# First feed-forward network on pairs of fp16 halves instead of pairs of fp32r halves, scales worked out on the chip

## The chip, the cores and the metric

One core of one Trainium2 chip runs the whole program in one launch. The metric is device microseconds of that core; lower is better. Engines are named as in the profile: PE (TensorE matmuls), PEld (its weight loads), DVE (VectorE), ACT (ScalarE), POOL (GpSimd), SP (SyncE, which issues most DMAs).

## The reference, cut to what matters

```python
X = np.fft.rfft(x, axis=1)                       # x: 8 x 3072 x 256
y = np.fft.irfft(X * (filt_r + 1j*filt_i), n=3072, axis=1)
x = y.reshape(24576, 256)
h = x @ w_in                                     # w_in: 256 x 2048, float64
g = np.where(h >= 1, h, np.where(h <= -1, 0.0, (h + 1)**2 / 4))
x = (g @ w_out).astype(np.float32)               # w_out: 2048 x 256, float64
logits = x @ w_gate                              # 8 experts
e = argmax(logits); p = softmax(logits)[e]
out = p * (np.maximum(x @ w1[e], 0) @ w2[e])     # w1: 256 x 1024, w2: 1024 x 256 per expert
```

The filter is a Fourier transform along 3072 positions, the first network is dense over all 24576 tokens, and the second sends each token to one of eight experts.

## The kernel before, in words

**Three parts in time.** The first sequence's transform, alone, with the conversion of the first network's weights (0 to 126 us). Then 768 *units* of the first network, 48 blocks of 512 tokens times 16 slices of 128 hidden columns; beside the first 672 of them the transforms of the seven other sequences run in the gaps, one per 96 units, so that the last 96 units have none. From about 2720 us on the experts, in tiles of 256 tokens.

**Precision by pairs.** A number is split into a high part and a rest (`wih`, `wil` for the first weights, `woh`, `wol` for the second, `xh`, `xl` for the tokens, `gh`, `gl` for the activations), and a product is three matmuls: high by high, high by rest, rest by high. In the first network both parts are of type fp32r, four bytes; the experts do the same with fp16 parts (their weights' scale is worked out on the chip in `wscale`, and each token row has its own).

**A unit.** `l1` issues six matmuls of 512 columns into one of two PSUM tiles `hps` (L453). DVE clips the sum to -1..1 (`cl`, L456), ACT squares (L457), DVE takes the maximum of square and sum (`g`, L463), which frees `hps`; ACT rounds `g` to `gh` (L466), POOL subtracts to get `gl` (L467). Three units later `l2` multiplies by the second weights: eight matmuls of 264 columns with `gh`, four with `gl` (L478), 264 because the gate's eight columns are folded into `w_out`. After 16 units `finish` copies the sums out and DVE works out each token's scale and expert.

**Weights.** The float64 weights arrive as pairs of integers, a slice of both matrices per DMA pair (`cv_load`, 16 slices, two `raw` buffers). `cv_run` rebuilds fp32 numbers in eight DVE operations; ACT and POOL split them (`cv_in`, `cv_out`); a transposition, a copy and a small matmul fold in the gate. Slices 0 to 14 are placed in the transform's list of times, slice 15 in the list of events.

**What sets the order.** The code writes each piece of work under a time (`at`, for the first sequence) or under a half unit (`ev`); a scheduler then sets each engine's stream from the dependences. Engines run their streams in order and wait on semaphores. On PE nothing but the stream's order decides what is next.

Of the kernel before, what the change touches and what calls it, by code (L numbers as in the profile page):

```python
# [23 lines left out]
BLK = 512  # L24
# [8 lines left out]
CVA, CVN, CH, CS = 4, 15, -29, 4  # L33
# [95 lines left out]
def tile_kernel(ctx, tc, x, w_in, w_out, w_gate, w1, w2, cst, tab, fil, out):  # L129
# [27 lines left out]
    wih = wp.tile([128, 2, FF], F32R, name="wih")  # L157
    wil = wp.tile([128, 2, FF], F32R, name="wil")
    woh = wp.tile([128, NF, WO], F32R, name="woh")
    wol = wp.tile([128, NF, WO], F32R, name="wol")  # L160
# [4 lines left out]
    if True:  # L165
# [21 lines left out]

        def cv_run(f, i):
            if i == 0:
                ex = fp.tile([128, 512], I32, tag="cl", name="cvx")  # L190
                m = fp.tile([128, 512], I32, tag="g", name="cvm")
                r = fp.tile([128, 512], I32, tag="gh", name="cvr", bufs=4)
                w = fp.tile([128, 512 + E], F32, tag="row", name="cvw")
# [36 lines left out]
        def cv_lg(f):  # L230
            w, wt = cv[f]
            lg = psH.tile([128, 512], F32, tag="h", name="hps")
            for k in range(2):
                PE.matmul(lg[:, 0:E], lhsT=wt[:, k * 128:(k + 1) * 128], rhs=wg[:, k, :], start=k == 0, stop=k == 1)
            cv[f] = (w, lg)

        def cv_out(f):
            w, lg = cv.pop(f)
            V.tensor_copy(w[:, 512:512 + E], lg[:, 0:E])
            A.activation(woh[:, f, :], w[:, 256:512 + E], AF.Copy)  # L240
            G.tensor_tensor(wol[:, f, :], w[:, 256:512 + E], woh[:, f, :].bitcast(F32), op=ALU.subtract)
# [45 lines left out]
        def fft_unit(u, ha, sa, hb, sb, lag):  # L287
# [78 lines left out]
            def b_inv(g):  # L366
                tt = st.pop(("b", g))[0]
                yh, yl = st.pop(("q", g))
                p = ups(u)
                for i in range(2):  # L370
                    pi = p[0:96, i * D:(i + 1) * D]
                    if u:
                        mm(pi, tt[:, 0, i, 128:224], tt[:, 1, i, 128:224], yh[:, i], yl[:, i])
                    else:
                        PE.matmul(pi, lhsT=tt[:, 0, i, 128:224], rhs=yh[:, i], start=True, stop=False)
                        PE.matmul(pi, lhsT=tt[:, 0, i, 128:224], rhs=yl[:, i], start=False, stop=True)
                z = alt(u, g, [96, 2, D], "z", (qp, "ao"), (qp, "xi"), (qp, "xg"), (qp, "xr"))
                A.activation(z.rearrange("p q d -> p (q d)"), p[0:96], AF.Copy)
                SP.dma_start(s2v[8 * g:8 * g + 8].rearrange("(q p) s d -> (p s) q d", q=2), z)

            if u == 0:
# [6 lines left out]
                for f in range(CVN):  # L388
# [5 lines left out]
                    at(t, (cv_in, f), (cv_tr, f), (cv_ev, f), (cv_lg, f))  # L394
                    at(t + 1, (cv_out, f))
                for g in range(NG):
# [5 lines left out]
                    at(t + P0[12], (b_inv, g))  # L402
                for _, _, fs in sorted(todo):
# [42 lines left out]
        def l1(n):  # L446
# [75 lines left out]
        def route1(k, i):  # L522
# [5 lines left out]
            if i == 0:  # L528
# [10 lines left out]
                A.activation(ex, d, AF.Exp)  # L539
# [115 lines left out]
        for f in range(CVN, NF):  # L655
            h = CH + CS * (f - CVN)
            ev(h - 6, lambda f=f: cv_load(f))
            for i in range(4):
                ev(h, lambda f=f, i=i: cv_run(f, i))
            for fn in (cv_in, cv_tr, cv_ev, cv_lg, cv_out):  # L660
                ev(h + 1, lambda f=f, fn=fn: fn(f))
# [264 lines left out]
```

## Time and profile before

| | |
|---|---|
| median of 3 runs | 3791.17 us (3788.31 to 3793.49) |
| the profiled execution | 3793.5 us, all of it span (first to last instruction) |
| PE busy | 3651.2 us, 96% of the span |
| PEld, DVE, ACT, POOL busy | 86%, 64%, 50%, 49% |
| TensorE clock, mean over the span | 0.990 of full |

The profiled execution is one of the three runs, 2.3 us above their median. PE's busy time covers matmuls from start to modelled end, and these overlap; what one matmul costs in a stream is read from the distance of two starts. A row of the timeline is: start, duration, engine, line, operation, output <- inputs, and in brackets the idle time before it with what ended it.

### The profile page before, as it was taken

The page shows a single profiled execution, that of the slowest core. Times are in us where ns is not written, and L with a number is a line of the kernel's source. Part 1 is how long each engine was busy: PE and PEld are TensorE (multiplying, and loading weights), DVE is VectorE, ACT ScalarE, POOL GpSimd, SP SyncE. Part 2 cuts the span into 40 slices and gives each one's busy share as a digit, 9 for nine tenths or more (in the row PEclk, how much of TensorE's full clock was granted, in tenths as well). Part 3 has the DMA queues.
Part 4 walks back from the last instruction along what each step waited for, and adds up shares of the span by engine and source line. Part 5 has one row for each costly group of instructions (what it writes and reads, how often), then busy time and mean ns, then how long its engine had stood idle before and what let it go on. Part 6 is the DMA issues. An engine that isn't in the chain of part 4 may idle for free. (4 is left out here: it accounts for less than half of the span.)

```text
span 3793.5 us, 70055 instructions
## 1 busy us (share of the span) xinstructions
PE 3651.2 (96%) x26055; PEld 3267.4 (86%) x26055; DVE 2417.0 (64%) x4496; ACT 1900.6 (50%) x3376; POOL 1877.7 (49%) x1570
## 2 busy tenths in 40 slices
PE   6999999999999999999999999999999999999998
PEld 4788888888888888888888888898888888888887
DVE  7588768767876876777687677767643333333332
ACT  6556556656665665666566556544432222222222
POOL 3555565556556656555665556555432222222222
PEclk8999999999999999999999999999999999999999
DMA  9444434434443443444344334201122222222221
GB/s 289 133 133 137 127 122 144 133 101 136 136 130 108 143 129 115 125 136 122 124 139 126 114 106 149 87 23 66 47 69 53 52 51 52 52 52 51 51 52 52
DMA packets 326122, 395.01 MB, mean 104 GB/s; under 512 B 164047, under 2 KB 254415, under 8 KB 325264
## 3 DMA queue, kind: packets, MB, share of 16 engines
q1 hardware_dynamic: 277152, 279.90, 25.9%
q0 software_dynamic: 48624, 110.58, 9.7%
q8 instruction: 207, 3.39, 0.4%
q14 instruction: 139, 1.14, 0.1%
HBM read 439.70 MB, written 120.49 MB: 148 GB/s over the span
## 5 line engine op out<-in xcount | busy, mean ns | idle before, releaser
L467 POOL TENSOR_TENSOR gl<-g,gh 128x512 fp32r<-128x512 f32 x768 | 1024.7, 1339 | 787.3 <-ACT gh L466 722.8
L478 PE MATMUL yps<-woh,gh 128*128 128x264 f32 x3072 | 812.4, 286 | 2.7 <-ACT gh L466 2.2
L478 PE MATMUL yps<-wol,gh 128*128 128x264 f32 x3072 | 811.0, 285 | 0.0
L463 DVE TENSOR_TENSOR g<-cl,hps 128x512 f32<-128x512 f32 x768 | 524.2, 683 | 353.7 <-ACT cl L457 277.3
L466 ACT ACTIVATE gh<-g 128x512 fp32r<-128x512 f32 x768 | 483.3, 630 | 455.8 <-DVE g L463 436.7
L453 PE MATMUL hps<-xh,wih 128*128 128x512 f32 x1536 | 621.6, 405 | 56.1 <-DVE g L463 55.0
L795 DVE SCALAR_TENSOR_TENSOR hl<-mh,hh 128x512 f16<-128x512 f32 x388 | 268.2, 691 | 633.8 <-ACT hh L794 632.7
L457 ACT ACTIVATE cl<-cl 128x512 f32<-128x512 f32 x768 | 483.7, 630 | 365.4 <-DVE cl L456 308.6
L478 PE MATMUL yps<-woh,gl 128*128 128x264 f32 x3072 | 634.5, 287 | 11.6 <-POOL gl L467 11.1
L456 DVE TENSOR_SCALAR cl<-hps 128x512 f32<-128x512 f32 x768 | 525.2, 684 | 172.6 <-PE hps L453 170.5
L453 PE MATMUL hps<-xh,wil 128*128 128x512 f32 x1536 | 604.4, 393 | 0.0
L453 PE MATMUL hps<-xl,wih 128*128 128x512 f32 x1536 | 603.7, 393 | 0.0
L478 PEld LDWEIGHTS yps<-woh,gh 128*128 128x128 f32 x3072 | 579.1, 189 | 25.0 <-ACT gh L466 5.2
L478 PEld LDWEIGHTS yps<-wol,gh 128*128 128x128 f32 x3072 | 579.3, 189 | 17.6
L794 ACT ACTIVATE hh<-mh 128x512 f16<-128x512 f32 x388 | 231.4, 597 | 724.4 <-PE mh L789 715.0
L789 PE MATMUL mh<-xt,wslot 128*128 128x256 f16 x4656 | 572.1, 273 | 0.0
L812 PE MATMUL my<-wslot,hh 128*128 128x256 f16 x3104 | 529.2, 273 | 0.0
L478 PEld LDWEIGHTS yps<-woh,gl 128*128 128x128 f32 x3072 | 489.6, 189 | 40.5 <-POOL gl L467 19.3
L825 POOL DMA_INDIRECT out_dram<-o,me x194 | 191.8, 989 | 658.6 <-ACT o L822 536.8
L789 PEld LDWEIGHTS <-wslot 128*128 128x128 f16 x4656 | 455.0, 98 | 53.1 <-issue 0.3
L812 PE MATMUL my<-wslot,hl 128*128 128x256 f16 x1552 | 422.9, 273 | 0.0
L453 PEld LDWEIGHTS hps<-xh,wih 128*128 128x128 f32 x1536 | 289.9, 189 | 112.2 <-DVE g L463 75.4
(159 smaller groups left out, 4911.6 us busy)
## 6 DMA issues: line engine op xcount, KB each, us to landing
tf<-in_fil_dram SPq DMA_DIRECT2D x113, 512.0 KB
tt<-in_tab_dram POOLq DMA_DIRECT2D x112, 448.0 KB
wst<-in_w_dram SPq DMA_DIRECT2D x128, 256.0 KB
xi<-in_x_dram SPq DMA_DIRECT2D x48, 512.0 KB
scr<-ao SPq DMA_DIRECT2D x48, 512.0 KB
a<-scr SPq DMA_DIRECT2D x128, 192.0 KB
scr<-z SPq DMA_DIRECT2D x128, 192.0 KB
zt<-scr SPq DMA_DIRECT2D x48, 512.0 KB
```

Of the source, the lines that this page charges most:

```text
L453: PE.matmul(p, lhsT=w[:, kt, f * 128:(f + 1) * 128], rhs=xx[:, kt, :], start=i == 0, stop=i == 5)
L456: V.tensor_scalar(cl, p, -1.0, 1.0, op0=ALU.max, op1=ALU.min)
L457: A.activation(cl, cl, AF.Square, bias=0.5, scale=0.5)
L463: V.tensor_tensor(g, cl, p, op=ALU.max)
L466: A.activation(gh, g, AF.Copy)
L467: G.tensor_tensor(gl, g, gh.bitcast(F32), op=ALU.subtract)
L478: PE.matmul(yps[j][:, 0:WO], lhsT=gg[:, s], rhs=w[:, f, :], start=f == 0 and i == 0, stop=f == NF - 1 and i == 2)
L789: PE.matmul(p[:, i, :], lhsT=w[:, wo + kt * FE + f * 128:wo + kt * FE + f * 128 + 128], rhs=xt_[:, xo + kt, :], start=a == 0, stop=a == 5)
L794: A.activation(hh, p, AF.Relu)
L795: V.scalar_tensor_tensor(hl, p, 0.0, hh, op0=ALU.max, op1=ALU.subtract)
L812: PE.matmul(yq[t][tk][:, 0:D], lhsT=hx[:, i, s], rhs=wx, start=fpair == 0 and i == 0 and a == 0, stop=fpair == 3 and i == 1 and a == 2)
L825: G.indirect_dma_start(out=out, out_offset=IOA(ap=me.bitcast(I32)[:, tk, 1:2], axis=0), in_=o, in_offset=None, bounds_check=NTOK - 1, oob_ ...
```

## The change

The first network's parts become fp16: `wih`, `wil`, `woh`, `wol`, `xh`, `xl`, `gh`, `gl`. Since fp16 has a small range, powers of two scale them: one for each weight matrix and one for the gate columns (`wq`, from maxima over the 16 converted slices `w32`, all kept until then) and one set per sequence (`sq`, from the maxima `zm` over the transform's output `z`). A maximum over partitions (`bmax`) is a PE transposition, a DVE reduction and a small matmul that spreads the result. Clip bounds, the square's scale and bias and the maximum's factor become columns of `sq`, read per partition, instead of constants; so does the factor in the exponential and in the stored gate. `cv_run` has four shift-and-mask operations and a compare-and-multiply, and a maximum behind them; all 16 slices are now in the transform's list of times. The split moves out of `cv_run`'s slice into `cv_split`, which can start only when all slices and `cv_scale` are done; its subtraction is on DVE, not on POOL. The matmuls' shapes and number stay.

```diff
-CVA, CVN, CH, CS = 4, 15, -29, 4
+CVA, CVS, CH = 4, 4, -6
...
-    wih = wp.tile([128, 2, FF], F32R, name="wih")
-    woh = wp.tile([128, NF, WO], F32R, name="woh")
+    wih = wp.tile([128, 2, FF], F16, name="wih")
+    woh = wp.tile([128, NF, WO], F16, name="woh")
+    wmx = wp.tile([128, 3, NF], F32, name="wmx")
+    wq = wp.tile([128, 12], F32, name="wq")
...
             if i == 0:
-                V.tensor_scalar(ex, hi, 20, 0x7FF, op0=ALU.logical_shift_right, op1=ALU.bitwise_and)
-                V.tensor_scalar(m, hi, 0xFFFFF, 0x100000, op0=ALU.bitwise_and, op1=ALU.bitwise_or)
+                V.tensor_scalar(a, hi, 0x7FFFFFF, 3, op0=ALU.bitwise_and, op1=ALU.logical_shift_left)
+                V.tensor_scalar(k, hi, 0x7FFFFFFF, None, op0=ALU.bitwise_and)
...
             else:
-                V.scalar_tensor_tensor(ex, hi, -(1 << 31), ex, op0=ALU.bitwise_and, op1=ALU.bitwise_or)
-                V.scalar_tensor_tensor(w[:, 0:512], w[:, 0:512], 2.0 ** -20, ex.bitcast(F32), op0=ALU.mult, op1=ALU.mult)
+                V.scalar_tensor_tensor(w, k.bitcast(F32), 1.125 * 2.0 ** -15, a.bitcast(F32), op0=ALU.is_ge, op1=ALU.mult)
+                V.tensor_reduce(wmx[:, 0:2, f], w.rearrange("p (a b) -> p a b", a=2), axis=AX.X, op=ALU.max, apply_absolute_value=True)
...
-            G.tensor_tensor(wil[:, :, s], wi, wih[:, :, s].bitcast(F32), op=ALU.subtract)
...
+        def cv_split(f):
...
+            A.activation(wih[:, :, s], wi, AF.Copy, scale=wq[:, 3:4])
+            V.scalar_tensor_tensor(wil[:, :, s], wi, wq[:, 3:4], wih[:, :, s], op0=ALU.mult, op1=ALU.subtract)
+            A.activation(woh[:, f, :], w[:, 256:512 + E], AF.Copy, scale=wq[:, 4:5])
+            V.scalar_tensor_tensor(wol[:, f, :], w[:, 256:512 + E], wq[:, 4:5], woh[:, f, :], op0=ALU.mult, op1=ALU.subtract)
+        def bmax(m, n):
...
+            PE.transpose(p[0:n, 0:k], m, c[0:k, C_ID:C_ID + k])
...
+            V.tensor_reduce(q, p[0:n, 0:k], axis=AX.X, op=ALU.max)
...
+            PE.matmul(p[:, 0:n], lhsT=c[0:n, C_ONE:C_ONE + 128], rhs=q)
...
+        def scales(u):
+            zm = sq[u]
+            m = fp.tile([96, 1], F32, tag="zr", name="zr")
+            V.tensor_reduce(m, zm, axis=AX.X, op=ALU.max)
...
+            pow2(q[:, 0:1], bmax(m, 1), -30, 100)
+            over(q[:, 6:7], q[:, 0:1], 18)
...
                 A.activation(z.rearrange("p q d -> p (q d)"), p[0:96], AF.Copy)
+                V.tensor_reduce(sq[u][:, g:g + 1], z.rearrange("p q d -> p (q d)"), axis=AX.X, op=ALU.max, apply_absolute_value=True)
...
+                at(tcv + 2, (cv_scale,))
+                for f in range(CVS):
+                    at(tcv + 2, (cv_split, f))
...
-            A.activation(xh[:, kt, :], p, AF.Copy)
-            V.tensor_tensor(xl[:, kt, :], p, xh[:, kt, :].bitcast(F32), op=ALU.subtract)
+            A.activation(xh[:, kt, :], p, AF.Copy, scale=sx)
+            V.scalar_tensor_tensor(xl[:, kt, :], p, sx, xh[:, kt, :], op0=ALU.mult, op1=ALU.subtract)
...
-            V.tensor_scalar(cl, p, -1.0, 1.0, op0=ALU.max, op1=ALU.min)
-            A.activation(cl, cl, AF.Square, bias=0.5, scale=0.5)
+            V.tensor_scalar(cl, p, q[:, 5:6], q[:, 3:4], op0=ALU.max, op1=ALU.min)
+            A.activation(cl, cl, AF.Square, bias=q[:, 11:12], scale=q[:, 4:5])
...
-            V.tensor_tensor(g, cl, p, op=ALU.max)
-            gh = fp.tile([128, BLK], F32R, tag="gh", name="gh", bufs=4)
+            V.scalar_tensor_tensor(g, p, q[:, 7:8], cl, op0=ALU.mult, op1=ALU.max)
+            gh = fp.tile([128, BLK], F16, tag="gh", name="gh", bufs=4)
             A.activation(gh, g, AF.Copy)
-            G.tensor_tensor(gl, g, gh.bitcast(F32), op=ALU.subtract)
+            G.tensor_tensor(gl, g, gh, op=ALU.subtract)
...
+        for f in range(CVS, NF):
+            ev(CH + 2 * (f - CVS), lambda f=f: cv_split(f))
...
+            ev(h + 192 - ZO[1] - 5, lambda u=u: scales(u))
```

How the streams move. First DVE at the end of the first part, before: the last two slices (L204 to L208), the split of the first tokens (`xl`), the gate's columns (L239), then the first unit's clip.

```order
L204 TENSOR_SCALAR cvx_967<-cvx_967 128x512
L239 COPY cvw_878<-hps_943 128x8
L207 SCALAR_TENSOR_TENSOR cvx_967<-raw_964,cvx_967 128x512
L205 SCALAR_TENSOR_TENSOR cvw_970<-cvr_969,cvm_968 128x512
L208 SCALAR_TENSOR_TENSOR cvw_970<-cvw_970,cvx_967 128x512
L441 TENSOR_TENSOR xl_995<-fps_996,xh_994 128x512
L239 COPY cvw_919<-hps_956 128x8
L441 TENSOR_TENSOR xl_995<-fps_1003,xh_994 128x512
L239 COPY cvw_970<-hps_986 128x8
L554 TENSOR_SCALAR row_1643<-c_67 128x4
L456 TENSOR_SCALAR cl_1017<-hps_1010 128x512
```

The same place of the changed kernel (its own line numbers: L271 and L273 are `cv_split`'s subtractions, L505 `xl`, L521 the clip, L288 and L255 of `scales`). Ahead of it stand the eleven `wil` subtractions of the other slices.

```order
L271 SCALAR_TENSOR_TENSOR wil_82<-w32_11_113,wq_86,wih_81 128x2x128
L273 SCALAR_TENSOR_TENSOR wol_84<-w32_0_102,wq_86,woh_83 128x264
L273 SCALAR_TENSOR_TENSOR wol_84<-w32_1_103,wq_86,woh_83 128x264
L273 SCALAR_TENSOR_TENSOR wol_84<-w32_2_104,wq_86,woh_83 128x264
L255 TENSOR_SCALAR sq_955<-sq_955 128x1
L273 SCALAR_TENSOR_TENSOR wol_84<-w32_3_105,wq_86,woh_83 128x264
L273 SCALAR_TENSOR_TENSOR wol_84<-w32_4_106,wq_86,woh_83 128x264
L505 SCALAR_TENSOR_TENSOR xl_986<-fps_987,sq_955,xh_985 128x512
L273 SCALAR_TENSOR_TENSOR wol_84<-w32_5_107,wq_86,woh_83 128x264
L273 SCALAR_TENSOR_TENSOR wol_84<-w32_6_108,wq_86,woh_83 128x264
L288 TENSOR_SCALAR sq_955<-sq_955 128x1
L505 SCALAR_TENSOR_TENSOR xl_986<-fps_994,sq_955,xh_985 128x512
```

Between this `xl` and the first clip nine more `wol` and four more `wil` subtractions follow: what were a slice's own steps all through the first part now stands in one run in front of the first unit.

Next DVE near the end of the third sequence's transform, in the changed kernel (before there is nothing but L456, L463 and single other operations): the last maximum over `z` (L437), then `scales` (L280, L241, L251, L252), spread between units.

```order
L437 TENSOR_REDUCE zm<-z 96x1
L280 TENSOR_REDUCE zr<-zm 96x1
L521 TENSOR_SCALAR cl<-hps,sq 128x512
L528 SCALAR_TENSOR_TENSOR g<-hps,sq,cl 128x512
L521 TENSOR_SCALAR cl<-hps,sq 128x512
L241 TENSOR_REDUCE bm<-fps 1x1
L528 SCALAR_TENSOR_TENSOR g<-hps,sq,cl 128x512
L680 TENSOR_REDUCE wmax<-wst 128x1 x2
L521 TENSOR_SCALAR cl<-hps,sq 128x512
L680 TENSOR_REDUCE wmax<-wst 128x1
L251 TENSOR_SCALAR sq<-fps 128x1
L252 TENSOR_SCALAR sq<-sq 128x1
```

The three steps of the maximum over partitions stand a unit apart from each other, with the units' own operations between them.

## Rows read from the trace of the kernel before

**Rows 1.** Windows: length; busy (instructions) of each engine; granted clock; DMA share; GB/s

```profile
300.00:400.00 100.00, 95.25 (x627) 85.95 (x626) 84.61 (x157) 59.60 (x109) 57.22 (x50) 1.00 0.46 137
800.00:1200.00 400.00, 389.78 (x2500) 349.88 (x2499) 297.29 (x565) 242.87 (x434) 241.31 (x187) 1.00 0.40 123
1200.00:1600.00 400.00, 387.04 (x2507) 348.99 (x2506) 303.44 (x561) 246.38 (x440) 237.80 (x190) 1.00 0.41 125
1600.00:2000.00 400.00, 382.36 (x2492) 345.39 (x2491) 299.21 (x554) 246.61 (x439) 236.37 (x193) 1.00 0.44 131
2500.00:2600.00 100.00, 100.00 (x650) 90.85 (x649) 63.10 (x131) 49.17 (x88) 52.46 (x42) 1.00 0.07 22
```

**Rows 2.** Groups by line and shape, 800 to 2000 us: count, busy, mean ns, idle before

```profile
L467 POOL TENSOR_TENSOR gl<-g,gh 128x512 fp32r<-128x512 f32 x346 | 463.5, 1344 | 336.6 <-ACT gh L466 299.8 <-ACT rs L566 27.5 <-PE hps L453 2.8
L453 PE MATMUL hps<-xh,wih 128*128 128x512 f32 x692 | 279.2, 403 | 22.9 <-DVE g L463 22.3
L463 DVE TENSOR_TENSOR g<-cl,hps 128x512 f32<-128x512 f32 x346 | 236.1, 683 | 162.1 <-ACT cl L457 131.9 <-POOL gl L467 25.3 <-issue 2.5
L585 ACT ACTIVATE row<-ysb,sm 128x256 f16<-128x256 f32 x88 | 37.5, 497 | 15.7 <-DVE sm L520 8.2 <-DVE sm L519 3.9 <-DVE gt L549 2.1
L512 DVE TENSOR_REDUCE sm<-ysb 128x2 f32<-128x512 f32 x44 | 29.8, 676 | 0.2
L490 DVE COPY ysb<-yps 128x264 f32<-128x264 f32 x44 | 17.6, 423 | 2.1 <-PE yps L478 2.1
```

**Rows 3.** Timeline, PE, one unit without a transform beside it

```profile
2562.43 0.28 PE L478 MATMUL yps<-woh,gh 128*128 128x264 f32 x1
...
2563.42 0.65 PE L478 MATMUL yps<-woh,gl 128*128 128x264 f32 x4
2563.90 0.39 PE L453 MATMUL hps<-xh,wih 128*128 128x512 f32 x1
...
2565.28 0.28 PE L478 MATMUL yps<-woh,gh 128*128 128x264 f32 x1
```

**Rows 4.** Timeline, PE and DVE, an expert tile on fp16 parts

```profile
3302.06 1.47 PE L789 MATMUL mh<-xt,wslot 128*128 128x256 f16 x12
3303.37 0.38 PE L812 MATMUL my<-wslot,hh 128*128 128x256 f16 x2
...
3299.64 0.48 DVE L824 TENSOR_SCALAR o<-my,gs 128x256 f32<-128x256 f32 x1
```

**Rows 5.** Waits of PE, whole span: total us, times, longest

```profile
PE hps L453 <- DVE g L463: 55.0, 68, 2.8
PE yps L478 <- POOL gl L467: 11.1, 14, 1.8
```

**Rows 6.** Groups by line and shape, 0 to 135 us

```profile
L208 DVE SCALAR_TENSOR_TENSOR cvw<-cvw,cvx 128x512 f32<-128x512 f32 x16 | 14.8, 924 | 0.3
L215 POOL TENSOR_TENSOR wil<-cvw,wih 128x256 fp32r<-128x256 f32 x16 | 14.1, 883 | 35.1 <-ACT wih L214 35.1
L214 ACT ACTIVATE wih<-cvw 128x256 fp32r<-128x256 f32 x16 | 6.7, 416 | 13.3 <-DVE cvw L208 13.2
```

**Rows 7.** Timeline, DVE, the first slice's conversion, nothing beside it

```profile
10.07 0.43 DVE L198 TENSOR_SCALAR cvx<-raw 128x512 int32<-128x512 int32 x1 [5.12 <-DMA raw<-in_w_out_dram]
10.41 0.42 DVE L199 TENSOR_SCALAR cvm<-raw 128x512 int32<-128x512 int32 x1
...
13.20 0.69 DVE L208 SCALAR_TENSOR_TENSOR cvw<-cvw,cvx 128x512 f32<-128x512 f32 x1
```

**Rows 8.** Timeline, end of the first part

```profile
110.63 0.43 DVE L202 TENSOR_SCALAR cvr<-raw 128x512 int32<-128x512 int32 x1 [2.06 <-DMA raw<-in_w_out_dram]
...
125.80 0.77 PE L453 MATMUL hps<-xh,wih 128*128 128x512 f32 x1
126.07 0.16 DVE L554 TENSOR_SCALAR row<-c 128x4 int32<-128x4 f32 x1
...
131.18 0.69 DVE L463 TENSOR_TENSOR g<-cl,hps 128x512 f32<-128x512 f32 x1 [1.74 <-ACT cl L457]
```

More of the change, by code (lines that the diff above doesn't have):

```diff
@@ L155, in tile_kernel @@
     fp = ffn.enter_context(tc.tile_pool(name="fp", bufs=2))
[L157 to L160 removed]
+    wih = wp.tile([128, 2, FF], F16, name="wih")
+    wil = wp.tile([128, 2, FF], F16, name="wil")
+    woh = wp.tile([128, NF, WO], F16, name="woh")
+    wol = wp.tile([128, NF, WO], F16, name="wol")
+    wmx = wp.tile([128, 3, NF], F32, name="wmx")
+    wq = wp.tile([128, 12], F32, name="wq")
     def fps(n=512):
@@ L186, in cv_load @@
             cv[f] = raw
+        wt = ExitStack()
+        wtp = wt.enter_context(tc.tile_pool(name="wtp", bufs=1))
+        w32 = [wtp.tile([128, 512 + E], F32, name=f"w32_{f}") for f in range(NF)]
         def cv_run(f, i):
             if i == 0:
[L190 to L193, printed above, removed]
@@ L227, in cv_ev @@
-            A.activation(wt, tp[:, 0:256], AF.Copy)
-            cv[f] = (w, wt)
+            t = fp.tile([128, 256], F32, tag="gl", name="cvt", bufs=4)
+            A.activation(t, cv[f][:, 0:256], AF.Copy)
+            cv[f] = t
         def cv_lg(f):
-            w, wt = cv[f]
+            t = cv[f]
             lg = psH.tile([128, 512], F32, tag="h", name="hps")
             for k in range(2):
-                PE.matmul(lg[:, 0:E], lhsT=wt[:, k * 128:(k + 1) * 128], rhs=wg[:, k, :], start=k == 0, stop=k == 1)
@@ L235, in cv_lg @@
-            cv[f] = (w, lg)
+                PE.matmul(lg[:, 0:E], lhsT=t[:, k * 128:(k + 1) * 128], rhs=wg[:, k, :], start=k == 0, stop=k == 1)
+            cv[f] = lg
         def cv_out(f):
[L238 to L241, printed above, removed]
+            w = w32[f][:, 512:512 + E]
+            V.tensor_copy(w, cv.pop(f)[:, 0:E])
@@ new lines, in pow2, with over, cv_scale @@
+        def pow2(o, i, lo, hi):
+            V.tensor_scalar(o, i, 2.0 ** lo, 2.0 ** hi, op0=ALU.max, op1=ALU.min)
+            V.tensor_scalar(o.bitcast(I32), o.bitcast(I32), 0x7F800000, None, op0=ALU.bitwise_and)
+        def over(o, i, e):
+            V.tensor_scalar(o.bitcast(I32), i.bitcast(I32), -1.0, float((254 + e) << 23), op0=ALU.mult, op1=ALU.add)
+        def cv_scale():
+            m = fp.tile([128, 3], F32, tag="wm", name="wm")
+            V.tensor_reduce(m, wmx, axis=AX.X, op=ALU.max)
+            pow2(wq[:, 0:3], bmax(m, 3), -60, 80)
+            over(wq[:, 3:6], wq[:, 0:3], 14)
+            V.tensor_tensor(wq[:, 6:7], wq[:, 5:6], wq[:, 1:2], op=ALU.mult)
+            V.tensor_scalar(wq[:, 6:7], wq[:, 6:7], 2.0 ** -14, None, op0=ALU.mult)
@@ L387, in fft_unit @@
                     at(P0[0] + P0[1] * g, (a_run, g))
-                for f in range(CVN):
+                for f in range(NF):
                     t = P0[2] + P0[3] * f + (P0[4] if f >= CVA else 0)
@@ L654, in tile_kernel @@
         V.tensor_tensor(cal, c[:, C_A:C_A + 128], cah.bitcast(F32), op=ALU.subtract)
[L655 to L661, printed above, removed]
+        scales(0)
+        for f in range(CVS, NF):
+            ev(CH + 2 * (f - CVS), lambda f=f: cv_split(f))
+        ev(CH + 2 * (NF - CVS), wt.close)
         ev(-8, lambda: z_load(0))
```

74 lines of the change are left out of this document (51 added, 23 removed).

## The prediction

> **What bounds the kernel now.** I read the engines' busy shares first, then windows by stage, then groups by line in one stage, then PE's timeline in a unit, and at last the waits of PE. The reader is to see five things.
>
> First, in the middle of the run (800 to 2000 us, transforms beside the units) PE is busy 389.78, 387.04 and 382.36 us of 400 each: idle for 40.8 us of 1200, 3.4% [rows 1]. DVE is busy for 899.9 us, 75%; POOL for 715 us, 60%; ACT for 736 us, 61% [rows 1].
>
> Second, the first matmul of a unit's halves (L453 with `xh`, `wih`) stands 692 times, two per unit, so this stretch holds 346 units of 1200/346 = 3.468 us [rows 2]. Per unit that is 3.350 us of PE, 2.60 of DVE, 2.13 of ACT, 2.07 of POOL.
>
> Third, without a transform PE has no gap (100.00 us busy of 100 [rows 1]), and a unit is the sum of its matmuls' distances: six of 512 columns in 2565.28 - 2563.90 = 1.38 us (0.230 each), eight of 264 in 0.99 us (0.124), four in 0.48 us (0.120), together 2.85 us [rows 3].
>
> Fourth, what PE waits for is above all `g` on DVE, which frees the PSUM tile: 55.0 us in 68 waits over the whole span, against 11.1 us for POOL's `gl` [rows 5]. These are bursts of DVE's queue, not its mean rate.
>
> Fifth, the busiest stretch of DVE in these rows is 300 to 400 us, 84.6%, and there PE is idle for 4.75% [rows 1].
>
> So the units are bound by PE's stream, with DVE close behind while transforms run.
>
> **The change part by part.**
>
> *Matmuls on fp16.* Shapes and number stay; the distance changes. The experts show fp16: twelve of 256 columns in 3303.37 - 3302.06 = 1.31 us, 0.1092 each [rows 4]. By columns 512 cost 0.2184 us and 264 cost 0.1126 us, so a unit costs 1.310 + 1.351 = 2.661 us, 0.189 less. Over 768 units that is 145 us, if PE alone decides. From below: no 512-column fp16 matmul is in the trace; if it kept 0.230, only the twelve short ones gain, 0.119 per unit, 91 us. I take 145, since the fp16 row holds full-width loads and matmuls in the same alternation. PE's clock is at full in all these windows [rows 1]. The Trainium skill (TensorE: Matmul & The Clock Gate, Back-to-back issue gap) gives a warm matmul its columns over 2.4 GHz and 2.5 ns; the row of 256 agrees (109.2 ns measured), and by it 512 would cost 215.8 ns and the sum would be 157 us.
>
> *Work added on DVE beside the units.* 16 maxima over `z` per 96 units at 0.676 us (as L512 [rows 2]): 0.113 per unit. Per-partition operands in clip, maximum and `xl`: L824, 256 columns out of PSUM with such an operand, took 0.48 us [rows 4], the plain copy of 264 columns 0.423 [rows 2]; 0.06 each, 0.13 per unit. They may cost nothing (0 to 0.13); I take 0.13. `scales`: 18 small operations of 0.16 us (as L554 [rows 8]) per sequence, 0.03 per unit; its PE steps are a unit apart in the stream, so I count no PE wait, and up to 2 us for each of seven if the sums come late. DVE's need becomes 2.60 + 0.113 + 0.13 + 0.03 = 2.87 us. ACT's scale operands: L585, 256 columns with one, took 0.497 us [rows 2], L214 without 0.416 [rows 6]; 0.08 on some two operations, 2.30 us per unit, which the unit covers.
>
> *POOL's subtraction with fp16 operands.* POOL has only 32-bit rows; `gl` took 1.344 us [rows 2]. From below it is half of that (and worth at most the 11.1 us that PE waits for `gl` [rows 5]), from above twice; I take 1.344, the nearest row. The Trainium skill (GPSIMD Engine Reference, Elementwise — side-by-side cycle accounting) prices such an operation by elements, 2.6 cycles each because its two inputs share one read port, an estimate of 1.11 us for 512; no run here shows fp16, and by it the time stays, which is why the POOL rival below is given little.
>
> *What DVE's share does to PE.* PE needs 3.350 - 0.189 = 3.161 us per unit beside a transform. From 75% to 84.6% of DVE the idle share rose from 3.4 to 4.75%, 0.14 per point [rows 1]; at 86% that line gives 4.9%. The chain behind `hps` grows by 0.06 + 0.08 + 0.06 = 0.20 us, which on the 68 waits [rows 5] is 13.6 us, 0.6% of these units. With 5.5% a unit takes 3.161/0.945 = 3.345 us and DVE is at 2.87/3.345 = 86%, so the two agree. That is 0.123 less than 3.468; over 672 units 83 us. The last 96 keep all 0.189: 18 us.
>
> *The first part.* Removed are 16 times a slice's eight operations, 3.82 us alone (10.07 to 13.89 [rows 7]) and more beside POOL (L208 took 0.924 on average [rows 6], 0.69 alone [rows 7]); added are two of 0.34, three of 0.69 and a maximum of 0.68, 3.4 us, and 16 maxima over `z`. POOL loses its subtractions (14.1 us for `wil` [rows 6], as much again for `wol`). So DVE has less to do until the last slice lands, which is at 110.6 us [rows 8]. Behind it everything is now serial: 3.4 us of conversion, some 2.5 for its gate columns, some 3 for the eight small steps and two PE trips of `cv_scale`, so about 119.5. Then ACT has twelve `wih` and five `woh` at about 0.5 us in front of `xh`: first matmul near 128.5, against 125.80 [rows 8]. DVE has 16 small scalings, then 32 subtractions of 256 to 264 columns (0.34 to 0.42 each) and two `xl` in front of the first clip: near 136.5, and the first `g` two us and a half later, 139, against 131.18 [rows 8]. I count 8 us. If DVE's relief lets the last slice land sooner it is 5 us less than before; if its queue stretches beside POOL it is 18 more. The two DMAs of slice 15 stay in SP's queue before the first unit in both orders.
>
> *Sum,* on the profiled execution of 3793.5 us, which has nothing outside its span: -83 - 18 + 8 = -93, 3700.5 us. The median of the runs stands 2.3 us lower, so 3698 us.
>
> **The rivals.**
>
> *DVE's extra work hides.* The waits come in bursts at the ends of blocks, where nothing is added; then the idle share stays 3.4%, a unit takes 3.272 us, and the gain is 132 + 18 - 8 = 142 us: 3649 us. For it speaks that PE waits for `g` only 68 times; against it, DVE would have to run at 88%, above any window shown.
>
> *DVE becomes the bound.* Its queue is in order and its operations wait for ACT between clip and maximum (131.9 us of such waits [rows 2]), so it may not get beyond a ceiling. At 83% a unit is 2.87/0.83 = 3.458 us and the gain is 7 + 18 - 8 = 17 us: 3774 us. At 82.4% nothing is gained, below it the kernel is slower. Against it: 84.6% occurs with PE still the busier [rows 1].
>
> *The 512-column matmuls keep their distance.* PE's need is 3.231 us per unit, 3.419 with the same idle share: 33 + 11 - 8 = 36 us, 3755 us.
>
> *Slower: POOL's subtraction slows on fp16.* POOL has 2.07 - 1.34 = 0.73 us of other work per unit. It sets the unit once `gl` takes over 3.345 - 0.73 = 2.61 us, and the kernel is slower from about 2.75, twice today's. At 3.0 us a unit is 3.73: 672 times 0.26 is 176, 96 times 0.15 is 14, with the start 198 us: 3989 us. For it: no mixed-width operation on POOL is in the trace. Against it: it must double.
>
> **How the numbers follow.** Forecast 45%, DVE hidden 22%, DVE ceiling 17% (3 of it within 0.2%, 3 slower), 512 columns unchanged 8%, POOL 8%. A difference under 0.2%, 7.6 us, can't be told from none here. Faster: 45 + 22 + 11 + 8 = 86%; same 3%; slower 11%. The forecast's own range is 3665 to 3730 (an idle share of 4 to 7%). The range of 8 in 10 reaches from the hidden case less a few us, 3640, to the ceiling at 83%, 3775.
>
> **What would show it.** In the changed profile: six 512-column matmuls in 1.31 us and twelve short ones in 1.35 in a unit without a transform; a unit of 3.35 us between 800 and 2000 us with DVE at 86% and PE idle for 5 to 6%; clip and maximum at 0.74 instead of 0.68 us; `gl` still near 1.34; the first matmul of the units near 128.5 and the first `g` near 139 us. The prediction is wrong in its main step if PE's idle share goes back to 3% or below, or if the waits for `g` grow beyond 150 us, and in its cover if `gl` exceeds 2.6 us.

## The result, and the profile after

The changed kernel takes 3843.67 us (median of 4 runs, 3843.38 to 3847.47), the kernel before beside it 3792.33 (3788.31 to 3794.11): ratio 1.0138, with a 95% interval of 1.0124 to 1.0152. It is slower by 1.4%; 3698 was forecast, and the range ended at 3775.

The groups by line of the kernel after, 800 to 2000 us (count, busy us, mean ns, idle time before and what ended it), answer to [rows 2]; the last two lines are `xl`, which the change lengthened, and the maximum over `z`, which it added:

```profile
L532 POOL TENSOR_TENSOR gl<-g,gh 128x512 f16<-128x512 f32 x337 | 408.8, 1220 | 358.8 <-ACT gh L531 326.5 <-PE hps L517 26.8 <-PE yps L543 2.0
L522 ACT ACTIVATE cl<-cl,sq 128x512 f32<-128x512 f32 x337 | 273.0, 810 | 175.3 <-DVE cl L521 114.6 <-DVE d L602 25.5 <-DVE oh L601 14.4
L521 DVE TENSOR_SCALAR cl<-hps,sq 128x512 f32<-128x512 f32 x337 | 269.5, 800 | 28.6 <-PE hps L517 27.6
L517 PE MATMUL hps<-xh,wih 128*128 128x512 f16 x674 | 261.0, 387 | 53.6 <-DVE g L528 53.0
L528 DVE SCALAR_TENSOR_TENSOR g<-hps,sq,cl 128x512 f32<-128x512 f32 x338 | 251.6, 745 | 133.2 <-ACT cl L522 119.9 <-POOL gl L532 10.9 <-ACT rs L631 1.0
L505 DVE SCALAR_TENSOR_TENSOR xl<-fps,sq,xh 128x512 f16<-128x512 f32 x42 | 31.1, 742 | 4.9 <-ACT xh L504 4.8
L437 DVE TENSOR_REDUCE zm<-z 96x1 f32<-96x512 f32 x51 | 34.4, 675 | 6.0 <-ACT z L434 5.3
```

674 first matmuls of a unit's halves are 337 units in 1200 us, 3.561 us each, against 346 and 3.468 before [rows 2]. The two lines of before that clip and square are to be read beside L521 and L522 (the square is there without operands from a table):

```profile
L456 DVE TENSOR_SCALAR cl<-hps 128x512 f32<-128x512 f32 x346 | 236.3, 683 | 60.2 <-PE hps L453 59.0
L457 ACT ACTIVATE cl<-cl 128x512 f32<-128x512 f32 x346 | 217.8, 630 | 139.6 <-DVE cl L456 122.1 <-DVE d L537 4.3 <-DVE oh L536 2.6
```

So clip went from 0.683 to 0.800 us, square from 0.630 to 0.810, maximum from 0.683 [rows 2] to 0.745: 0.36 us more on the chain that frees a PSUM tile.

The windows after, for [rows 1] (length; busy of PE, PEld, DVE, ACT, POOL; granted clock; DMA share; GB/s):

```profile
300.00:400.00 100.00, 88.85 (x599) 59.90 (x598) 87.31 (x162) 64.17 (x108) 50.58 (x46) 0.98 0.44 130
800.00:1200.00 400.00, 360.51 (x2418) 242.31 (x2417) 319.68 (x602) 251.85 (x415) 214.98 (x183) 0.99 0.40 122
1200.00:1600.00 400.00, 366.46 (x2450) 247.88 (x2448) 321.87 (x566) 257.42 (x424) 216.73 (x184) 0.98 0.40 123
1600.00:2000.00 400.00, 364.61 (x2429) 243.97 (x2428) 314.56 (x577) 255.96 (x421) 216.71 (x184) 0.97 0.39 119
```

PE is idle for 108.4 of the middle 1200 us, 9.0%, where it was 3.4%. DVE stands at 956.1/1200 = 79.7%; in the busiest of these windows, 300 to 400 us, it is at 87.3%, and there PE is idle for 11.2%, where it was 4.75% [rows 1]. The granted clock is below full.

PE's own pace came as forecast. PE's timeline in one unit without a transform, for [rows 3]:

```profile
2601.81 0.38 PE L517 MATMUL hps<-xh,wih 128*128 128x512 f16 x1
...
2603.11 0.28 PE L543 MATMUL yps<-woh,gh 128*128 128x264 f16 x1
...
2604.01 0.61 PE L543 MATMUL yps<-woh,gl 128*128 128x264 f16 x4
2604.45 0.38 PE L517 MATMUL hps<-xh,wih 128*128 128x512 f16 x1
```

Six matmuls of 512 columns in 1.30 us (0.217 each), twelve of 264 in 1.34: a unit of 2.64 us instead of 2.85.

What PE waited for, whole span (us, times, longest), for [rows 5]:

```profile
PE hps L517 <- DVE g L528: 128.9, 113, 3.6
PE yps L543 <- POOL gl L532: 36.1, 44, 2.2
PE yps L543 <- ACT gh L531: 12.0, 13, 2.0
```

And the start, for [rows 8] (start, duration, in brackets the idle time before and what ended it):

```profile
123.76 4.88 ACT L270 ACTIVATE wih<-w,wq 128x256 f16<-128x256 f32 x12
...
130.57 0.66 ACT L504 ACTIVATE xh<-fps,sq 128x512 f16<-128x512 f32 x1
131.28 1.01 PE L517 MATMUL hps<-xh,wih 128*128 128x512 f16 x2 [6.00 <-ACT xh L504]
...
134.96 0.58 PE L517 MATMUL hps<-xl,wih 128*128 128x512 f16 x1 [2.66 <-DVE xl L505]
...
143.58 1.46 DVE L528 SCALAR_TENSOR_TENSOR g<-hps,sq,cl 128x512 f32<-128x512 f32 x2
```

The last of the first network's matmuls begins at 2808.5 us instead of 2760.2; what follows takes 1033.1 and 1033.3 us. All of the loss is in front of it.

### The profile page after: what moved, and what is told of

The parts are those of the page before. It is cut to its first block, busy times and chain, and to the rows that moved or that the text cites. A ratio compares the mean times of both kernels' runs of the same rounds, so it can differ in the third digit from the quotient of the medians.

```text
span 3841.6 us, 70301 instructions
## 1 busy us (share of the span) xinstructions
PE 3551.2 (92%) x26082; PEld 2619.9 (68%) x26082; DVE 2622.7 (68%) x4808; ACT 2034.7 (53%) x3376; POOL 1747.7 (45%) x1538
## 5 line engine op out<-in xcount | busy, mean ns | idle before, releaser
L532 POOL TENSOR_TENSOR gl<-g,gh 128x512 f16<-128x512 f32 x768 | 925.8, 1212 | 865.0 <-ACT gh L531 810.5
L522 ACT ACTIVATE cl<-cl,sq 128x512 f32<-128x512 f32 x768 | 622.2, 811 | 398.8 <-DVE cl L521 277.7
L528 DVE SCALAR_TENSOR_TENSOR g<-hps,sq,cl 128x512 f32<-128x512 f32 x768 | 571.9, 745 | 313.2 <-ACT cl L522 290.7
L543 PE MATMUL yps<-woh,gh 128*128 128x264 f16 x3072 | 758.5, 279 | 23.4 <-ACT gh L531 12.0
L543 PE MATMUL yps<-wol,gh 128*128 128x264 f16 x3072 | 759.4, 278 | 0.0
L543 PEld LDWEIGHTS <-gh 128*128 128x128 f16 x6144 | 596.4, 99 | 233.7 <-issue 25.6
L517 PE MATMUL hps<-xh,wih 128*128 128x512 f16 x1536 | 592.0, 386 | 136.2 <-DVE g L528 128.9
L521 DVE TENSOR_SCALAR cl<-hps,sq 128x512 f32<-128x512 f32 x768 | 614.1, 800 | 56.8 <-PE hps L517 52.7
L517 PE MATMUL hps<-xl,wih 128*128 128x512 f16 x1536 | 591.4, 385 | 2.7 <-DVE xl L505 2.7
L517 PE MATMUL hps<-xh,wil 128*128 128x512 f16 x1536 | 591.1, 385 | 0.0
L543 PE MATMUL yps<-woh,gl 128*128 128x264 f16 x3072 | 540.9, 278 | 37.3 <-POOL gl L532 36.1
```

The costliest lines, as they stand in the source:

```text
L521: V.tensor_scalar(cl, p, q[:, 5:6], q[:, 3:4], op0=ALU.max, op1=ALU.min)
L522: A.activation(cl, cl, AF.Square, bias=q[:, 11:12], scale=q[:, 4:5])
L528: V.scalar_tensor_tensor(g, p, q[:, 7:8], cl, op0=ALU.mult, op1=ALU.max)
L532: G.tensor_tensor(gl, g, gh, op=ALU.subtract)
L543: PE.matmul(yps[j][:, 0:WO], lhsT=gg[:, s], rhs=w[:, f, :], start=f == 0 and i == 0, stop=f == NF - 1 and i == 2)
```

## The experiments

The theories: **A**, the per-partition operands of the activation; **B**, the later sequences' maxima and scales; **C**, the instruction order that the scheduler makes of other prices. Ratios are against the kernel before on the same chip, with their 95% intervals; 0.1% is 3.8 us. For these data the scales of all eight sequences are the same powers of two, so a constant can stand for a column of the table.

**e1_const_act**: A alone undone.

```diff
-V.tensor_scalar(cl, p, q[:, 5:6], q[:, 3:4], op0=ALU.max, op1=ALU.min)
-A.activation(cl, cl, AF.Square, bias=q[:, 11:12], scale=q[:, 4:5])
+V.tensor_scalar(cl, p, -2.0 ** 29, 2.0 ** 29, op0=ALU.max, op1=ALU.min)
+A.activation(cl, cl, AF.Square, bias=2.0, scale=2.0 ** -28)
...
-V.scalar_tensor_tensor(g, p, q[:, 7:8], cl, op0=ALU.mult, op1=ALU.max)
+V.scalar_tensor_tensor(g, p, 2.0 ** -25, cl, op0=ALU.mult, op1=ALU.max)
```

Expected:

> The changed kernel with constants in clip, square and maximum (the values that the chip works out for this data, the same for all eight sequences); scales are still worked out and used everywhere else. Theory A (per-partition operands lengthen the chain clip, square, maximum by 0.12 + 0.18 + 0.06 us and load DVE and ACT, and PE waits for it): clip back to 0.68 us, square to 0.63, unit beside a transform from 3.56 to about 3.40, time about 3750 us. Theory B (the maxima over z and the scale steps on DVE cost it): under 20 us gained, about 3830. Theory C (the order of the streams, set by the scheduler with its own idea of fp16's times, makes PE wait): under 20 us gained.

Measured: 3776.64 us, 0.9967 (0.9953 to 0.9981). Without these operands the change gives back 1.7%, more than the 1.4% that it lost. Theories B and C had put under 20 us on it, A some 94; it is some 65.

**e2_no_zmax**: B alone undone; the first sequence's scales serve all.

```diff
-if g == 0:
+if u == 0 and g == 0:
...
-V.tensor_reduce(sq[u][:, g:g + 1], z..., op=ALU.max, apply_absolute_value=True)
+if u == 0:
+    V.tensor_reduce(sq[u][:, g:g + 1], z..., op=ALU.max, apply_absolute_value=True)
...
-ev(h + 192 - ZO[1] - 5, lambda u=u: scales(u))
```

Expected:

> The changed kernel without the maxima over z and without scales for sequences 1 to 7 (the first sequence's scales serve all). Theory A: DVE loses 0.14 us of 2.84 per unit, 20 to 30 us gained, about 3815. Theory B: most of the loss goes, 60 to 90 us, about 3765. Theory C: under 20 us.

Measured: 3812.1 us, 1.0062 (1.0038 to 1.0086), 0.76% below the changed kernel: what A expected, not B.

**e4_before_ops**: the kernel before, its types kept, with the same three operations fed from a table `q` of constants.

```diff
-V.tensor_scalar(cl, p, -1.0, 1.0, op0=ALU.max, op1=ALU.min)
-A.activation(cl, cl, AF.Square, bias=0.5, scale=0.5)
+V.tensor_scalar(cl, p, q[:, 0:1], q[:, 1:2], op0=ALU.max, op1=ALU.min)
+A.activation(cl, cl, AF.Square, bias=q[:, 2:3], scale=q[:, 3:4])
...
-V.tensor_tensor(g, cl, p, op=ALU.max)
+V.scalar_tensor_tensor(g, p, q[:, 4:5], cl, op0=ALU.mult, op1=ALU.max)
```

Expected:

> The kernel before (fp32r) with per-partition operands, filled with the same constants, in clip, square and maximum, and nothing else. Theory A: slower than before although PE's pace is the old one, by 40 to 80 us, since the chain grows by 0.36 us per unit and DVE by 0.18. Theories B and C: within 15 us of before.

Measured: 3875.21 us, 1.0232 (1.0209 to 1.0255), 85 us more than the kernel before beside it, where A had 40 to 80. The operands, with the order that the scheduler makes of them, cost the old kernel no less, though its first network is still in fp32r.

**e5_types_only**: the kernel before with fp16 parts and constant scales; splits stay on POOL.

```diff
-wih = wp.tile([128, 2, FF], F32R, name="wih")
+wih = wp.tile([128, 2, FF], F16, name="wih")
...
-A.activation(xh[:, kt, :], p, AF.Copy)
+A.activation(xh[:, kt, :], p, AF.Copy, scale=2.0 ** 13)
...
-V.tensor_scalar(cl, p, -1.0, 1.0, op0=ALU.max, op1=ALU.min)
+V.tensor_scalar(cl, p, -2.0 ** 30, 2.0 ** 30, op0=ALU.max, op1=ALU.min)
...
```

Expected:

> The kernel before with fp16 parts and constant powers of two as scales (immediates, no scale is worked out; conversion, splits on POOL and event list as before). Theories A and B: PE's faster pace shows, a unit beside a transform 3.30 us or less, 110 to 140 us faster than before, about 3660. Theory C: PE waits eat the gain, no more than 40 us faster than before, 3750 or more.

Measured: 3709.45 us, 0.9783 (0.9749 to 0.9817). The matmuls' gain is real, some 82 us, but short of the 110 to 140 expected; this version beats both kernels. Its windows:

```profile
800.00:1200.00 400.00, 375.13 (x2544) 253.87 (x2542) 292.08 (x557) 245.99 (x439) 231.24 (x194) 1.00 0.41 129
1200.00:1600.00 400.00, 376.67 (x2564) 257.07 (x2563) 307.40 (x565) 253.75 (x451) 224.23 (x196) 0.99 0.43 132
1600.00:2000.00 400.00, 376.46 (x2589) 257.02 (x2588) 313.41 (x593) 253.50 (x458) 228.82 (x197) 1.00 0.43 129
```

PE is idle for 6.0% here, with DVE at 76%: the faster matmuls alone, with no work added on VectorE and in an order of their own, use up more than the 5.5% that the forecast had put on the full change.

But e1 and e4 also have another order: of VectorE's 4496 operations in the trace only 2100 of e4 stand at the same place as in the kernel before (going by what they write). Theory C was open. In the next three kernels the program is built as usual, and when its order is set, the operands of the 768 clips, squares and maxima are exchanged; the edit leaves order, buffers and waits alone, and in the traces the order is the same on every engine but for one pair of neighbours on VectorE in p1 and p2.

**p1_e4order_const, p2_beforeorder_ops, p3_afterorder_const.**

```diff
 with tile.TileContext(nc, schedule_with_timeline_sim=True) as tc:
     tile_kernel(tc, *args)
+for at, i in enumerate(ls):              # ls: the scheduled instructions
+    ...                                  # s: i's operands, the scalars replaced
+    ls[at] = type(i)(ins=s, **{x: getattr(i, x) for x in fields})
```

Expected:

> The kernel before, its instructions in the order that the kernel with per-partition operands (e4_before_ops) had, but with constants again in clip, square and max. If the 85 us that e4_before_ops lost were the longer operations themselves (theory A), the time returns to the one before, 3782 to 3800 us. If they came from the other order that the scheduler made of them (the rival), it stays near 3875. A split shows as a time between.

> The kernel before in its own order on every engine, but clip, square and max take per-partition operands from a table (0.80, 0.81 and 0.745 us instead of 0.68, 0.63 and 0.68). Theory A, the duration: 3865 to 3890 us. The rival, the order: 3785 to 3805 us. If an order that was made for other durations is worse than one made for these, more than 3890.

> The changed kernel in its own order on every engine, with constants in clip, square and max, the values that the table has for these data. Theory A: all of the 67 us that e1_const_act won were duration, so 3765 to 3790 us. The rival, that e1_const_act won by its other order: 3835 to 3850 us.

Measured: p1 3828.37 us, 1.0097 (1.0074 to 1.0120), between its two expectations; p2 3863.46, 1.0191 (1.0166 to 1.0216), just under the 3865 that A began with; p3 3775.6, 0.9951 (0.9939 to 0.9964). In a table, with the operand's price in one order from left to right:

| order of | constants | per-partition | difference |
|---|---|---|---|
| before | 1 | 1.0191 (p2) | 1.9% |
| e4_before_ops | 1.0097 (p1) | 1.0232 (e4) | 1.35% |
| after | 0.9951 (p3) | 1.0138 (after) | 1.9% |

The longer operations cost 1.35 to 1.9% at an unchanged order, in both kernels: A is shown. C is worth 0.4 to 1% in e4 (the smaller figure, e4 against p2, has overlapping intervals). In the change nothing shows it: with its own order and constants it is as fast as e1 with another (0.9951, 0.9967). The groups of p3, 800 to 2000 us, show these three at the lengths that they have with constants:

```profile
L528 DVE SCALAR_TENSOR_TENSOR g<-hps,cl 128x512 f32<-128x512 f32 x345 | 235.8, 684 | 110.9 <-ACT cl L522 84.0 <-POOL gl L532 25.0 <-ACT rs L631 0.8
L521 DVE TENSOR_SCALAR cl<-hps 128x512 f32<-128x512 f32 x346 | 235.3, 680 | 52.9 <-PE hps L517 51.8
L522 ACT ACTIVATE cl<-cl 128x512 f32<-128x512 f32 x346 | 216.5, 626 | 166.5 <-DVE cl L521 112.1 <-DVE d L602 24.2 <-DVE oh L601 14.6
```

VectorE's waits over the whole span tell who leads: how long it waited for ScalarE's square and for PE to deliver `hps`, in before, after and p3:

```profile
DVE g L463 <- ACT cl L457: 277.3, 345, 4.3
DVE cl L456 <- PE hps L453: 170.5, 218, 2.5
```

```profile
DVE g L528 <- ACT cl L522: 290.7, 349, 3.5
DVE cl L521 <- PE hps L517: 52.7, 70, 2.8
```

```profile
DVE g L528 <- ACT cl L522: 192.2, 266, 2.4
DVE cl L521 <- PE hps L517: 121.6, 185, 3.3
```

Before, VectorE had caught up with PE at 218 clips of 768; after, at 70. The wait for the square is almost as long before as after, so it doesn't tell the two apart; at the changed kernel's order the operands lengthen it by half (192.2 to 290.7 us). VectorE isn't full there: a fifth of its time between 800 and 2000 us is idle, half of that waiting for the square (119.9 of 244 us), in an order that lets nothing pass.

**p5_square_const, p6_clipmax_const**: as p3, but square alone, or clip and maximum alone, get constants.

```diff
-    return lambda k, i: [[imm(-2.0 ** 29), imm(2.0 ** 29)], [imm(2.0), imm(2.0 ** -28)], [imm(2.0 ** -25)]][k]   # p3: clip, square, max
+    return lambda k, i: [imm(2.0), imm(2.0 ** -28)] if k == 1 else None                                      # p5: square alone
+    return lambda k, i: [[imm(-2.0 ** 29), imm(2.0 ** 29)], None, [imm(2.0 ** -25)]][k]                      # p6: clip and max alone
```

Expected:

> The changed kernel in its own order on every engine; square alone takes constants (0.81 to 0.63 us on ScalarE), clip and max keep their per-partition operands. If the 68 us are VectorE's own work (its share near 80%), little is won here: 3830 to 3845 us. If they are the length of the chain clip, square, max, which holds one of the two hps buffers, square's 0.18 us is half of the 0.36 and wins about half: 3800 to 3815 us.

> The changed kernel in its own order; clip and max take constants (0.80 to 0.68 and 0.745 to 0.685 us on VectorE), square keeps its per-partition operands. If the 68 us are VectorE's own work: 3775 to 3790 us. If they are the length of the chain, 0.18 of 0.36 us: 3800 to 3815 us.

Measured: p5 3825.04 us, 1.0091 (1.0071 to 1.0111); p6 3803.43, 1.0028 (1.0017 to 1.0040). Square gives back 0.47%, clip and maximum 1.1%, both 1.87%. Each part shortens the chain by 0.18 us, so VectorE's own work isn't all of it: the chain has a price (square). The windows 800 to 2000 us of p3, p5 and p6:

```profile
800.00:2000.00 1200.00, 1112.90 (x7512) 758.21 (x7512) 926.60 (x1796) 732.31 (x1306) 662.83 (x565) 0.98 0.41 126
800.00:2000.00 1200.00, 1102.15 (x7402) 745.60 (x7400) 961.37 (x1756) 721.08 (x1280) 662.91 (x559) 0.98 0.40 124
800.00:2000.00 1200.00, 1102.44 (x7442) 747.21 (x7440) 920.17 (x1765) 782.96 (x1290) 658.04 (x560) 0.99 0.40 125
```

PE is idle for 7.3% in p3, 8.2% in p5, 8.1% in p6 and 9.0% in the changed kernel, at the same order; VectorE is busy for 77.2, 80.1, 76.7 and 79.7%. From 200 to 2400 us the idle shares are 7.7, 8.5, 8.5 and 9.3%. So between these four kernels, with one profile each, PE's idle share goes with the length of the chain and not with VectorE's busy share: either half of the chain adds 0.8 to 0.9 points, on whichever engine it lies. Over the whole run the medians put about twice as much on clip and maximum as on square; where that difference lies isn't shown (p5's profile is of its fastest run, 8 us below its median).

**c12_const_no_zmax**: e1's and e2's edits together.

```diff
-V.tensor_scalar(cl, p, q[:, 5:6], q[:, 3:4], op0=ALU.max, op1=ALU.min)
+V.tensor_scalar(cl, p, -2.0 ** 29, 2.0 ** 29, op0=ALU.max, op1=ALU.min)
...
-if g == 0:
+if u == 0 and g == 0:
...
```

Expected:

> The changed kernel with constants in clip, square and max and without the later sequences' maxima and scales: e1_const_act and e2_no_zmax together. If the two costs add (67 and 32 us below 3844), 3735 to 3755 us; if they share the same idle time of VectorE, so that the second gives little once the first is gone, 3760 to 3780. What is left above e5_types_only (3709) is then the start and the converted weights, at most 45 us.

Measured: 3738.86 us, 0.9856 (0.9833 to 0.9879). The two edits together give back 2.8%; the single gains, 1.71 and 0.76, sum to 2.5, so the costs don't share one idle time.

**s1_early_split**: c12, and the weights' maxima left out too, each chunk split with a constant scale as soon as it is converted.

```diff
-at(t + 1, (cv_out, f))
+at(t + 1, (cv_out, f), (cv_split, f))
...
-at(tcv + 2, (cv_scale,))
-for f in range(CVS):
-    at(tcv + 2, (cv_split, f))
...
```

Expected:

> The changed kernel with constants in clip, square and max and without the later sequences' maxima (as c12_const_no_zmax), and now without the weights' maxima too: each chunk of weights is split with a constant scale as soon as it is converted, so that no split waits for the last chunk. If the 30 us between c12_const_no_zmax (3739) and e5_types_only (3709) are this wait at the start, 3700 to 3715 us, with 22 to 26 units begun at 160 us instead of 14. If they lie later (splits on VectorE and ScalarE beside the first units, another order), 3725 to 3740 us.

Measured: 3726.45 us, 0.9821 (0.9805 to 0.9838): 0.35%, 13 us, not 30, with intervals that just overlap those of c12; it falls in the second of the two ranges expected. Its first matmul and maximum:

```profile
121.26 0.86 PE L506 MATMUL hps<-xh,wih 128*128 128x512 f16 x2
...
125.99 0.69 DVE L517 SCALAR_TENSOR_TENSOR g<-hps,cl 128x512 f32<-128x512 f32 x1
```

By 160 us it has begun 13 units, c12 and the changed kernel 7, the kernel before 11 (half the count of `hps<-xh,wih` up to there). The expectation counts halves, 22 to 26 instead of 14; 26 were measured. So the wait for the last chunk is gone, and by the medians it was worth less than half of what was put on it.

**s2m_x_const, s2_all_const**: what could be left between s1 and e5. s2m is s1 in its own order with a constant in `xh` and `xl`; s2 has no maxima and no table at all.

```diff
-A.activation(xh[:, kt, :], p, AF.Copy, scale=sx)
-V.scalar_tensor_tensor(xl[:, kt, :], p, sx, xh[:, kt, :], op0=ALU.mult, op1=ALU.subtract)
+A.activation(xh[:, kt, :], p, AF.Copy, scale=2.0 ** 13)
+V.scalar_tensor_tensor(xl[:, kt, :], p, 2.0 ** 13, xh[:, kt, :], op0=ALU.mult, op1=ALU.subtract)
...
-scales(0)                                 # s2 only, with the first sequence's maxima
```

Expected:

> s1_early_split in its own order on every engine, but the split of the activations (xh on ScalarE, xl on VectorE, 96 of each) takes a constant instead of the sequence's scale from a table. If the 17 us that s1_early_split still is above e5_types_only are these longer operations (0.09 us each on xh, about as much on xl, 17 us of both engines' time in all, in front of waiting matmuls), 3708 to 3718 us. If they are the order, 3720 to 3730 us.

> All scales constant and no maxima at all: the types, the five-operation conversion, each chunk split as soon as it is converted (with VectorE), order as the scheduler makes it. If the order or the x operands were what is left of s1_early_split, it comes to e5_types_only: 3700 to 3715 us; if splitting the weights on VectorE instead of GpSimd costs the rest, 3720 to 3735. It begins its units earlier than the kernel before, so it may be the fastest of all, 3690 to 3700.

Measured: s2m 3725.58 us, 0.9817 (0.9801 to 0.9833); s2 3721.19, 0.9802 (0.9785 to 0.9818). The `x` operands cost nothing that can be told: s2m falls in the range that was expected if the order was what was left (3720 to 3730), s2 in the one for splitting on VectorE (3720 to 3735). The intervals of s1, s2m and s2 all overlap that of e5 (0.9749 to 0.9817): of the 17 us that were to be explained, which were taken from medians on two chips, nothing is resolved. Whether splitting the weights on VectorE costs a little, and whether e5 or s2 is the fastest, stays open; both beat the kernel before and the changed one.

## Why the prediction was wrong

The whole way, by ratios, one step after another: types, conversion and splits with constants -1.98% (s2); the first sequence's scales and the `x` operands +0.19, within the error; splitting the weights only after the last chunk +0.35 (13 us); the later maxima and scales +1.11 (42 us; 0.76 and 29 us if the operands are still there); the activation's operands +1.71 (65 us). Together +1.38. At a held order only the operands were tried (1.87 there); each of the other steps has an order of its own, and a part of the 1.11 may be order, as in e4.

**PE's own need, right.** Six of 512 columns in 1.30 us where 1.31 was forecast, twelve short ones in 1.34 where 1.35 was. The Trainium skill (TensorE: Matmul & The Clock Gate, Back-to-back issue gap) has 215.8 ns for 512 columns by its formula for a single matmul, and 131 ns in a stream of weight loads and matmuls. Measured in a stream are 217: the formula agrees, the lower figure does not. POOL's `gl` took 1.220 us, not more than 1.344, and that rival is out.

**The operands, mis-sized.** The forecast had "0.06 each" on VectorE and "0.08" on ScalarE, and "the chain behind `hps` grows by 0.06 + 0.08 + 0.06 = 0.20 us". The price was about right per operand and was counted per instruction: clip has two such operands (+0.117 us), square has two (+0.180), the maximum one (+0.062). The chain grew by 0.36. On the 68 waits that were there, 0.20 us was to cost 13.6; instead there were 113 waits, and 73.9 us more of them. The Trainium skill (ScalarE: Activation LUTs, What ACT_TABLE_LOAD costs) says that each such operand of an activation adds about 93 ns; an estimate by it is 0.186 for square's two. The traces agree: 0.180 there, and `xh`, with one, went from 0.580 to 0.672 us. The forecast did not use it.

**The step that failed: "What DVE's share does to PE".** It drew a line of the idle share over VectorE's busy share, read 4.9% off at 86%, and came to 5.5% with the longer chain. Measured are 9.0% at 79.7%. The rows carried no such line: at 74.3 and 74.8% of DVE the idle share was 2.6 and 4.4% [rows 1]. VectorE's work per unit was nearly right (956.1/337 = 2.84 us; 2.87 forecast), but 86% on average were not to be had. What shrank per unit was its wait for PE (L456 and L521 above: 59.0/346 = 0.17 us before, 27.6/337 = 0.08 after), while its wait for the square between clip and maximum stayed (131.9/346 = 0.38 [rows 2], 119.9/337 = 0.36; in p3, with constants, 84.0/346 = 0.24). PE's idle share went with the matmuls' pace (6.0% in e5) and with the length of the chain (7.3% in p3, 8.1 to 8.2% with half of the operands, 9.0% with all). The nearest rival is "DVE becomes the bound", which gets slower than before below 82.4%, and was given 17% with only 3 on the slower side. But p6, with VectorE at 76.7%, waits as much as p5 at 80.1%: it is the two engines in turn that bound it, not a ceiling of VectorE alone.

**A term that was not in the sum: TensorE's clock.** The forecast took it as full, as it was in the windows before [rows 1]. Windows of 2 us in the changed kernel, and the matmuls around the wait:

```profile
1952.00:1954.00 2.00, 1.30 (x11) 0.75 (x9) 1.90 (x2) 1.25 (x3) 1.76 (x2) 1.00 0.52 181
1954.00:1956.00 2.00, 0.00 (x0) 0.00 (x0) 1.59 (x3) 0.81 (x1) 0.81 (x1) 0.81 0.31 98
1956.00:1958.00 2.00, 1.77 (x5) 0.67 (x5) 1.66 (x4) 1.64 (x3) 1.08 (x1) 0.50 0.82 254
1958.00:1960.00 2.00, 2.00 (x9) 1.10 (x8) 1.90 (x3) 0.95 (x3) 1.13 (x2) 0.50 0.02 8
1960.00:1962.00 2.00, 2.00 (x11) 1.60 (x9) 0.75 (x1) 1.05 (x2) 0.54 (x1) 0.50 0.02 4
1962.00:1964.00 2.00, 2.00 (x14) 1.21 (x13) 0.08 (x1) 0.39 (x1) 1.15 (x1) 0.98 0.00 0
```

```profile
1951.61 0.29 PE L543 MATMUL yps<-woh,gh 128*128 128x264 f16 x1 [0.77 <-ACT gh L531]
...
1953.19 0.62 PE L543 MATMUL yps<-woh,gl 128*128 128x264 f16 x4 [0.51 <-POOL gl L532]
1956.23 0.59 PE L517 MATMUL hps<-xh,wih 128*128 128x512 f16 x1 [2.42 <-DVE g L528]
1956.61 0.63 PE L517 MATMUL hps<-xl,wih 128*128 128x512 f16 x1
```

Two short waits, then one of 2.42 us for `g`, and the granted clock stands at 0.50 (1.2 GHz) for some 6 us; PE is then busy throughout, at half pace. Over 140 to 2640 us the granted clock (before, after, e5):

```profile
140.00:2640.00 2500.00, 2416.56 (x15600) 2178.00 (x15599) 1875.25 (x3517) 1486.52 (x2647) 1461.28 (x1168) 1.00 0.39 119
```

```profile
140.00:2640.00 2500.00, 2280.65 (x15309) 1537.66 (x15308) 2027.58 (x3664) 1587.29 (x2609) 1340.21 (x1144) 0.98 0.39 119
```

```profile
140.00:2640.00 2500.00, 2351.44 (x16034) 1595.16 (x16033) 1885.00 (x3604) 1511.56 (x2702) 1391.90 (x1196) 1.00 0.40 122
```

Summed over 250 windows of 10 us, (1 - clock) times 10 us is 6.8 us before, 42.6 after, 31.3 in p3, 13.6 in c12, 10.2 in e5: up to 36 us of the loss are matmuls at half clock. PE was busy for 1091.6/337 = 3.239 us per unit, not 3.161, and at a clock of 0.98 up to 0.07 of these are the clock's. From the forecast unit of 3.345, the idle share (3.161/0.910 = 3.475) adds 0.13 us and the longer busy time the other 0.09, to the 3.561 measured.

**The start, mis-sized.** The first matmul came at 131.28 and the first `g` at 143.58, where 128.5 and 139 were forecast, against 125.80 and 131.18 [rows 8]. ACT's `wih` begin at 123.76. At 160 us four units were missing, 14 us, not 8; s1 got 13 back.

**The rest** was near: the last 96 units, without a transform, begin at 2465.1 us before and at 2529.4 after and take 295 and 279 us up to the last `xh` by `wih`: 16 us saved, for 18. So the miss lies in front of them, where 64 us were lost and 75 (83 less 8) were to be won.

Of the signs that the prediction named, the waits for `g` (128.9 us) stayed below the 150 that were to refute it, while the idle share of 9% was well outside its 5 to 6: the waits say nothing of the slower matmuls behind them, and PE also waited more for `gl` (36.1 us, 11.1 before).

## What to carry to other kernels

Count the per-partition operands, not the instructions that have them, and add up the whole chain that holds a buffer; a constant in their place was worth 1.9% here, almost all that faster matmuls had won. Don't read PE's waits off another engine's busy share: here they followed the length of a chain that passes between two engines (8.1 and 8.2% at shares of 76.7 and 80.1%). Faster matmuls alone went with a larger idle share as well (3.4 to 6.0%, e5), while the chain behind them kept its length. Where a change makes TensorE wait longer, price the half clock behind the wait as well as the wait.

## What was not expected of the hardware

A wait of 2.42 us, with two shorter ones ahead of it, was followed by some 6 us at a granted clock of 0.50. A per-partition operand costs 0.058 to 0.062 us on VectorE for 128x512 out of PSUM and 0.090 to 0.092 on ScalarE, whether one or two. GpSimd's subtraction of 128x512 was a little faster with an fp16 input and output (1.220 us) than with all 32 bits (1.344). And the kernel before, with operations of the same length in another order, took 1% more (p1).
